# Moving the adds of complex products from VectorE into accumulating matmuls, with wider table operations and a new load order, in a state-space layer with a gated unit

## The chip, the cores and the metric

The kernel runs on one core of one Trainium2 chip. The metric is the device time of one execution in microseconds (us); medians of several executions are quoted. Engines: PE is TensorE (PEld is its weight loads), DVE is VectorE, ACT is ScalarE, POOL is GpSimd, SP issues transfers.

## The reference

A layer norm, a diagonal state-space convolution over 2048 steps for 512 channels with 128 complex states, a residual, then a second layer norm and a gated unit (ReGLU) with its residual. What matters here:

```python
logdA = dt * A                      # A, B, C complex, [512, 128]
P = exp(logdA[:, :, None] * l)      # 2048 powers
K = einsum("dn,dnl,dn->dl", C, P, dt * B).real     # the convolution's kernel
y = irfft(rfft(pad(u)) * rfft(pad(K)))[:2048] + u * Dskip
h = x + y
h2 = h + (relu(n(h) @ W_gate) * (n(h) @ W_up)) @ W_down   # n: layer norm
```

The transforms are matrix products in stages. So the work has a **front** (load and normalize x, form tables of exp, sine and cosine, form the kernel K, transform u and K, multiply the spectra) and a **back** (last stage of the inverse transform, then the gated unit).

## The kernel before

The program collects its operations, and a list scheduler inside it (below, "the planner") fixes the order of each engine's instructions from prices of its own before anything is built. So every edit of an operation can move all others.

**Powers** (called in 8 blocks). A table V of 32 complex powers is made by doubling: from m powers come the next m, by a complex factor. Each level is two products and two adds on DVE:

```python
m = 1
while m < 32:
    src, dst, tmp = V[:, :, 0:m], V[:, :, m:2 * m], self.Vt[:, :, 0:m]
    s.tt(tmp, src, bc(zi), ALU.mult, "vB")
    s.tt(dst, src, bc(zr), ALU.mult, "vA")
    s.tt(dst[:, 0], dst[:, 0], tmp[:, 1], ALU.subtract, "vC")
    s.tt(dst[:, 1], dst[:, 1], tmp[:, 0], ALU.add, "vD")
    m *= 2
```

**Kernel generator** (16 units U). The table E (magnitude times sine or cosine, four products of 1024 elements a unit on DVE) meets V in 64 small matmuls:

```python
for dl in range(8):
    for ri in range(2):
        for d in range(4):
            c = 32 * (U % 2) + 8 * d + dl
            it.append((t.v(...), V[:, ri, :, c], E[:, ri, 8 * d + dl, :], ...))
s.mms(it, "kgen")
```

**Spectral product and first inverse step** (4 groups g, each in two halves of the frequencies):

```python
s.tt(Ta, Uv, Kv[:, :, 0].unsqueeze(2).to_broadcast([128, 64, 2, 16]), ALU.mult, "pA")
s.tt(Tb, Uv, Kv[:, :, 1].unsqueeze(2).to_broadcast([128, 64, 2, 16]), ALU.mult, "pB")
s.tt(Kv[:, :, 0], Ta[:, :, 0], Tb[:, :, 1], ALU.subtract, "pC")
s.tt(Kv[:, :, 1], Ta[:, :, 1], Tb[:, :, 0], ALU.add, "pD")
# ... then, for 8 columns j and two halves of the output:
it += [(o, Sv[:, 0, j], self.G1[:, 0, sl], True, False),     # Sv is the product in Kh
       (o, Sv[:, 1, j], self.G1[:, 1, sl], False, True)]     # 128 wide
s.evac(Zv[:, 64 * ih:64 * ih + 64, :, J0:J0 + 8], ..., "e_i1")
```

**Second inverse step.** Its stationary operand (the weights that PE loads) is a slice of Z, laid out `[128, 64, 2, 128]`:

```python
it.append((t.v(...), self.Z[:, i, ri], self.H[:, i, ri], False, q == 3 and ri == 1))
```

Of the kernel before, what the change touches and what calls it, by code (L numbers as in the profile page):

```python
# [8 lines left out]
FP32 = mybir.dt.float32  # L9
# [5 lines left out]
SB_BYTES = 207 * 1024  # L15
# [52 lines left out]
class Op:  # L68
    __slots__ = ("i", "engs", "cost", "body", "deps", "reads", "writes", "tiles", "tag", "tset",
                 "prio", "users", "eng", "start", "fin", "idx", "dma", "nbytes", "vc", "ndep", "sem", "wtiles",  # L70
                 "bias")


class Sched:
# [147 lines left out]
    def cost_act(self, n):  # L222
        return 185 + n * 0.833

    def cost_dve(self, n, rate):
        return 75 + n * rate
# [37 lines left out]
    def ts(self, out, a, s1, s2, op0, op1=None, tag="ts", engs=("dve",)):  # L264
# [3 lines left out]
        c = {"dve": self.cost_dve(n, r), "pool": 300 + n * 2.2}  # L268
# [18 lines left out]
    def mms(self, items, tag="mm"):  # L287
# [3 lines left out]
        for out, l, r, st, sp in items:  # L291
            n = free_elems(r)
            m = free_elems(l)
            c += max(n, 64) * 0.42 + (40 if m == 128 else 2 + 0.42 * m) * 0.7
            ins += [l, r]
            outs.append(out)
# [37 lines left out]
    def schedule(self):  # L334
        ops = self.ops
        LAT = 130.0
        for o in ops:
            o.users = []
            o.ndep = len(o.deps)
        for o in ops:  # L340
            for j in o.deps:
                ops[j].users.append(o)
            for t in o.tiles:
                t.left += 1
        for o in reversed(ops):
# [4 lines left out]
        for o in ops:  # L350
            o.prio += o.bias
# [57 lines left out]
        while n < len(ops):  # L409
# [29 lines left out]
            if cand is None:  # L439
                for o in ready["pe"][:3]:  # L440
                    for tl in o.wtiles:
                        print(o.tag, o.i, [(d.tag, d.i, {ops[j].tag: ops[j].i for j in d.deps if ops[j].eng is None}) for d in getattr(tl, "war", [])])
# [46 lines left out]
    def emit(self):  # L489
# [44 lines left out]
        for e in ("pool", "sp", "act", "dve", "pe"):  # L534
# [12 lines left out]
            starters[e](run)  # L547
L, D, N, F = 2048, 512, 128, 1376
# [3 lines left out]
def make_consts():  # L552
# [25 lines left out]
    g1 = np.zeros((64, 2, 2, 64, 2, 2))  # L578
    for g in range(2):
        g1[:, g, 0, :, 0, g] = np.cos(ph)  # L580
        g1[:, g, 0, :, 1, g] = np.sin(ph)
        g1[:, g, 1, :, 0, g] = -np.sin(ph)
        g1[:, g, 1, :, 1, g] = np.cos(ph)
    g1 = g1.reshape(128, 512)
# [14 lines left out]
    small = np.zeros((128, 128 + 128 + 128))  # L599
    small[:, 0:128] = np.eye(128)  # L600
    small[:, 128:256] = 1.0 / 512
    small[:, 256:384] = 1.0
# [5 lines left out]
class Kernel:  # L608
    def __init__(self, nc, I, out):
        self.nc, self.I, self.out = nc, I, out  # L610
        with ExitStack() as es:  # L611
# [10 lines left out]
            s.schedule()  # L622
# [3 lines left out]
    def layout(self):  # L626
# [8 lines left out]
        rC = reg(2 * (256 + 512 + 384))  # L635
# [4 lines left out]
        rVt = reg(4096)  # L640
        rMag = reg(16384)
        rTrig = reg(12288)
        rVz = reg(12288)
        rE = reg(16384)
        rS = reg(24576)
# [3 lines left out]
        rDsk = reg(1024)  # L649
# [3 lines left out]
        c = s.mem(rC, [128, 256 + 512 + 384], BF16)  # L653
        self.cc = c
        self.F1 = c[:, 0:256]
        self.G1 = c[:, 256:768].rearrange("p (r x) -> p r x", r=2)
        self.ident = c[:, 768:896]
        self.mean_w = c[:, 896:1024]
        self.ones = c[:, 1024:1152]
# [8 lines left out]
        self.Z = s.mem(rZ, [128, 64, 2, 128], BF16)  # L668

        self.V = [s.mem(rV + 8192 * i, [128, 2, 32, 64], BF16) for i in range(2)]  # L670
        self.Vt = s.mem(rVt, [128, 2, 16, 64], BF16)
        self.mag = [s.mem(rMag + 4096 * i, [128, 2, 32, 32], BF16) for i in range(4)]
        self.trig = [s.mem(rTrig + 6144 * i, [128, 3, 32, 32], BF16) for i in range(2)]
        self.vz = s.mem(rVz, [128, 12, 512], BF16)
        self.E = [s.mem(rE + 8192 * i, [128, 2, 32, 64], BF16) for i in range(2)]
        self.Eoff = [rE + 8192 * i for i in range(2)]
        self.S = [s.mem(rS + 8192 * i, [128, 32, 2, 64], BF16) for i in range(3)]
        self.Kh = [s.mem(rS + 8192 * i, [128, 32, 4, 2, 16], BF16) for i in range(3)]
        self.Tm = [s.mem(rT + 4096 * i, [128, 64, 2, 16], BF16) for i in range(2)]
# [3 lines left out]
        self.dsk = s.mem(rDsk, [128, 512], BF16)  # L683
        self.sm = rSm
        self.rS = rS
        self.par = s.mem(rT, [128, 6, 4, 128], BF16)
        self.ldt_b = s.mem(rT + 6144, [128, 512], BF16)
# [13 lines left out]
        assert rMag + 16384 - rV >= 32768  # L701
# [13 lines left out]
    def loads(self):  # L715
# [4 lines left out]
        s.generic("pool", 300, lambda e: e.memset(self.neghalf, -0.5), [self.neghalf], [], "ms")  # L720
        for g in range(2):
# [3 lines left out]
        for i, nm in enumerate(("A_A_re", "A_A_im", "A_B_re", "A_B_im", "A_C_re", "A_C_im")):  # L725
# [4 lines left out]
            if i == 1:  # L730
                s.dma(self.cc, self.cd["f1g1"][:], 128 * 2304, "cc")
# [20 lines left out]
    def prep(self):  # L752
# [8 lines left out]
        f = [s.mem(self.rS + 2048 * i, [128, 512], FP32) for i in range(12)]  # L761
# [39 lines left out]
        s.tt(self.vz[:, 0], t0, t1, ALU.add, "prep")  # L801
        s.tt(t0, wr, ms, ALU.mult, "prep")
        s.tt(t1, wp, mc, ALU.mult, "prep")
        s.tt(self.vz[:, 1], t0, t1, ALU.subtract, "prep")
# [3 lines left out]
        for m in range(5):  # L808
# [5 lines left out]
            s.evac(self.vz[:, 2 + 2 * m], br, "zcp")  # L814
            s.evac(self.vz[:, 3 + 2 * m], bi, "zcp")
# [63 lines left out]
    def vblock(self, B):  # L879
# [3 lines left out]
        s.evac(V[:, :, 0, :], self.vz[:, 0:2, sl], "v0")  # L883
        m = 1
        lev = 0
        while m < 32:
            zr = self.vz[:, 2 + 2 * lev, sl]
            zi = self.vz[:, 3 + 2 * lev, sl]

            def bc(z):  # L890
                return z.unsqueeze(1).unsqueeze(1).to_broadcast([128, 2, m, 64])
            src, dst, tmp = V[:, :, 0:m], V[:, :, m:2 * m], self.Vt[:, :, 0:m]
            s.tt(tmp, src, bc(zi), ALU.mult, "vB")
            s.tt(dst, src, bc(zr), ALU.mult, "vA")
            s.tt(dst[:, 0], dst[:, 0], tmp[:, 1], ALU.subtract, "vC")
            s.tt(dst[:, 1], dst[:, 1], tmp[:, 0], ALU.add, "vD")
            m *= 2
            lev += 1
# [12 lines left out]
    def tables_trig(self, U):  # L911
# [7 lines left out]
        s.act(tr[:, 0], t.v(), AF.Sin, tag="sin")  # L919
        s.act(tr[:, 2], t.v(), AF.Sin, bias=self.halfpi, tag="cos")  # L920
        s.ts(tr[:, 1], tr[:, 0], -1.0, None, ALU.mult, tag="neg")

    def etab(self, U):
# [4 lines left out]
        for ri in range(2):  # L928
# [196 lines left out]
```

## Time and profile before

| | before |
|---|---|
| time, median of 3 | 385.9 us (385.58 to 386.04) |
| span of the profiled execution | 384.3 us, mean granted PE clock 0.897 |
| front (to the start of the second inverse step at 239.8 us) | DVE busy 204.0, ACT 166.0, PE 129.0 |
| back (from there to the end) | PE busy 133.8 of 144.5 |

The page's first part gives busy time, share of the span and instruction count of each engine; its second part cuts the span into 40 slices and prints the busy share in tenths; its fourth part gives the shares of the chain of waits that ended last.

```profile
PE 262.8 (68%) x2885; PEld 163.4 (43%) x2904; DVE 266.9 (69%) x482; ACT 205.1 (53%) x249; POOL 5.2 (1%) x10
...
PE   0210052648445778673878599999999999999990
...
DVE  1599999999999546999999983755532741630803
...
PEclk9999999999755588985889769999999999999996
...
DVE 46%; PE 39%; issue 4%; DMA 3%; ACT 2%; ACTq 2%; POOLq 0%; POOL 0%; DVEq 0%
```

DVE is nearly full up to the 24th slice, PE from there on. In the front PE has gaps, and from the 11th to the 24th slice its granted clock reads 0.5 to 0.8 in most slices; in the first ten, where PE is nearly idle in half of them, it reads 0.9 or more.

### The profile page before, as it was taken

The page shows a single profiled execution, that of the slowest core. Times are in us where ns is not written, and L with a number is a line of the kernel's source. Part 1 is how long each engine was busy: PE and PEld are TensorE (multiplying, and loading weights), DVE is VectorE, ACT ScalarE, POOL GpSimd, SP SyncE. Part 2 cuts the span into 40 slices and gives each one's busy share as a digit, 9 for nine tenths or more (in the row PEclk, how much of TensorE's full clock was granted, in tenths as well). Part 3 has the DMA queues.
Part 4 walks back from the last instruction along what each step waited for, and adds up shares of the span by engine and source line. Part 5 has one row for each costly group of instructions (what it writes and reads, how often), then busy time and mean ns, then how long its engine had stood idle before and what let it go on. Part 6 is the DMA issues. An engine that isn't in the chain of part 4 may idle for free.

```text
span 384.3 us, 6840 instructions
## 1 busy us (share of the span) xinstructions
PE 262.8 (68%) x2885; PEld 163.4 (43%) x2904; DVE 266.9 (69%) x482; ACT 205.1 (53%) x249; POOL 5.2 (1%) x10
## 2 busy tenths in 40 slices
PE   0210052648445778673878599999999999999990
PEld 0100030326322454531768498845445544544540
DVE  1599999999999546999999983755532741630803
ACT  0256749989866378678899458443321320511201
POOL 0110000110000000000000000000000000000000
PEclk9999999999755588985889769999999999999996
DMA  5457000014450000000024981300000010010101
GB/s 129 136 162 281 6 0 1 2 25 95 96 228 0 0 2 0 3 1 0 3 90 159 367 342 33 118 0 2 0 3 0 20 36 0 18 39 2 39 17 55
DMA packets 21246, 24.10 MB, mean 63 GB/s; under 512 B 12928, under 2 KB 18656, under 8 KB 20448
## 3 DMA queue, kind: packets, MB, share of 16 engines
q1 hardware_dynamic: 20160, 22.62, 18.0%
q10 hardware_dynamic: 1056, 1.05, 0.8%
q8 instruction: 23, 0.38, 0.4%
q14 instruction: 7, 0.06, 0.0%
HBM read 17.37 MB, written 4.19 MB: 56 GB/s over the span
## 4 chain that ended last, share of the span: by engine, by line
DVE 46%; PE 39%; issue 4%; DMA 3%; ACT 2%; ACTq 2%; POOLq 0%; POOL 0%; DVEq 0%
PE psum L301 39%; DVE arena L261 37%; DVE arena L239 4%; DMA arena<-in_A_u_dram 3%; ACTq L327 2%; ACT arena L252 1%; DVE arena L821 1%; DVE arena L281 1%; DVE arena L272 1%; DVE arena L273 1%; PE psum L316 1%; ACT arena L238 1%; POOLq L611 0%; POOL arena L828 0%; ACT L252 0%
## 5 line engine op out<-in xcount | busy, mean ns | idle before, releaser
L301 PE MATMUL psum<-arena 128*32 128x64 bf16 (+6 forms) x2797 | 255.2, 274 | 90.8 <-DVE arena L261 45.7
L301 PEld LDWEIGHTS psum<-arena 128*128 128x128 bf16 (+3 forms) x2816 | 157.9, 128 | 188.1 <-DVE arena L261 46.5
L261 DVE TENSOR_TENSOR arena<-arena 128x1024 bf16<-128x1024 bf16 (+7 forms) x283 | 156.1, 606 | 3.8 <-ACT arena L238 1.2
L252 ACT ACTIVATE arena<-psum 128x1024 bf16<-128x1024 f32 (+2 forms) x92 | 72.2, 825 | 73.9 <-PE psum L301 70.5
L238 ACT ACTIVATE arena<-psum 128x1024 bf16<-128x1024 f32 (+2 forms) x89 | 77.9, 917 | 49.3 <-PE psum L301 29.3
L261 DVE TENSOR_TENSOR arena<-psum,arena 128x512 bf16<-128x512 f32 (+2 forms) x52 | 34.9, 688 | 47.5 <-PE psum L301 47.5
L239 DVE CAST arena<-psum 128x512 bf16<-128x512 f32 (+1 forms) x29 | 27.1, 947 | 30.3 <-PE psum L301 30.3
L252 ACT ACTIVATE arena<-arena 128x512 f32<-128x512 f32 (+3 forms) x25 | 18.1, 769 | 30.3 <-DVE arena L261 16.5
L316 PE MATMUL psum<-arena 128*128 128x128 bf16 x88 | 8.2, 243 | 21.5 <-DMA arena<-in_A_A_im_dram 13.5
L252 ACT ACT_TABLE_LOAD x12 | 15.4, 1283 | 9.9 <-issue 9.7
L821 DVE BATCH_NORM_STATS2 arena<-arena 128x6 f32<-128x512 bf16 x16 | 10.7, 683 | 12.2 <-DMA arena<-in_A_u_dram 12.2
L252 ACT ACTIVATE arena<-psum,arena 128x1024 bf16<-128x1024 f32 x16 | 17.5, 1116 | 1.7 <-DVE arena L261 1.7
L316 PEld LDWEIGHTS psum<-arena 128*128 128x128 bf16 x88 | 5.8, 106 | 23.4 <-DMA arena<-in_A_A_im_dram 13.5
L261 DVE TENSOR_TENSOR arena<-arena,psum 128x2048 bf16<-128x2048 bf16 x4 | 9.2, 2288 | 4.6 <-PE psum L301 4.6
L281 DVE SCALAR_TENSOR_TENSOR arena<-psum,arena 128x512 bf16<-128x512 f32 x16 | 11.1, 743 | 0.1
L238 ACT ACTIVATE arena<-arena 128x512 bf16<-128x512 f32 (+1 forms) x15 | 7.6, 518 | 5.7 <-PE psum L301 3.4
L239 DVE COPY arena<-psum 128x512 bf16<-128x512 bf16 x10 | 3.8, 410 | 9.7 <-PE psum L316 9.7
L272 DVE TENSOR_SCALAR arena<-arena 128x1024 bf16<-128x1024 bf16 (+1 forms) x20 | 7.1, 370 | 2.1 <-ACT arena L252 2.0
L828 POOL TENSOR_TENSOR arena<-arena 128x4 f32<-128x4 f32 x4 | 4.8, 1209 | 76.0 <-DVE arena L272 76.0
L273 DVE TENSOR_SCALAR arena<-arena 128x512 bf16<-128x512 bf16 x16 | 5.5, 410 | 0.0
L281 DVE SCALAR_TENSOR_TENSOR arena<-arena 128x512 f32<-128x512 f32 (+1 forms) x9 | 4.0, 446 | 0.2 <-POOL arena L828 0.2
L823 DVE BATCH_NORM_AGGREGATE arena<-arena 128x2 f32<-128x6 f32 x16 | 2.5, 174 | 0.3
(9 smaller groups left out, 2.5 us busy)
## 6 DMA issues: line engine op xcount, KB each, us to landing
arena<-const_h SPq DMA_DIRECT2D x4, 1024.0 KB, 5.8
arena<-const_m SPq DMA_DIRECT2D x4, 768.0 KB, 11.1
arena<-arena SPq DMA_DIRECT2D x32, 64.0 KB, 2.1
xd_spill<-arena SPq DMA_DIRECT2D x1, 2048.0 KB, 8.6
arena<-xd_spill SPq DMA_DIRECT2D x1, 2048.0 KB, 16.5
out_dram<-arena SPq DMA_DIRECT2D x16, 128.0 KB
arena<-in_B_W_gate_dram SPq DMA_DIRECT2D x1, 1376.0 KB, 8.8
arena<-in_B_W_up_dram SPq DMA_DIRECT2D x1, 1376.0 KB, 11.8
```

The lines of the kernel that those rows point to most:

```text
L238: return eng.activation(ap_of(out), ap_of(src), AF.Copy)
L239: return eng.tensor_copy(ap_of(out), ap_of(src))
L252: return eng.activation(ap_of(out), ap_of(src), func, **kw)
L261: return eng.tensor_tensor(ap_of(out), ap_of(a), ap_of(b), op)
L272: return eng.tensor_scalar(ap_of(out), ap_of(a), s1, s2, op0)
L273: return eng.tensor_scalar(ap_of(out), ap_of(a), s1, s2, op0, op1)
L281: return eng.scalar_tensor_tensor(ap_of(out), ap_of(a), s, ap_of(b), op0, op1)
L301: ins_ = eng.matmul(ap_of(out), l, r, start=st, stop=sp)
L316: r = eng.transpose(ap_of(out), i_, ident)
L327: return e.dma_start(out, src)
L821: s.generic("dve", 620, lambda e, k=k: e.bn_stats(self.st[:, k, :], self.x[:, k, :]), [self.st[:, k, :]], [self.x[:, k, :]], "bns")
L828: s.generic("pool", 600, lambda e, sl=sl: e.tensor_tensor(self.rs[:, sl], self.rs[:, sl], self.neghalf.to_broadcast([128, 4]), ALU.pow), [ ...
```

## The change

Its intent: DVE bounds the front, so take work from it.

- The last doubling writes its two products into two buffers (V and a new T2) and never adds them; the kernel generator runs twice as many matmuls, which accumulate both in PSUM.
- The spectral product writes both products, of all frequencies and half the columns at a time, and never adds them; the first inverse step runs four matmuls of 256 columns for each j in place of four of 128.
- The first doubling is done once for all blocks, the other adds are one instruction a level, the tables are two products of 2048 in place of four of 1024.
- The planner gets new prices and a list of priorities; among other things it decides the order of the loads.
- Z becomes `[128, 128, 128]` with the other index innermost.
- To make room, the spectra of K (S and Kh) have two buffers in place of three, and parameters and scratch share memory with other buffers.

The core of the diff (cuts marked):

```diff
     def cost_dve(self, n, rate):
-        return 75 + n * rate
+        return 155 + n * rate
...
-            s.schedule()
+            s.schedule(PRIO)
...
-        self.Z = s.mem(rZ, [128, 64, 2, 128], BF16)
+        self.Z = s.mem(rZ, [128, 128, 128], BF16)
...   (last doubling)
+            s.tt(V[:, m:2 * m]..., V[:, 0:m]..., zr, ALU.mult, "vA")
+            s.tt(self.swap(self.T2[:, m:2 * m]), V[:, 0:m], zi, ALU.mult, "vT")
...   (tables)
-        for ri in range(2):
-            s.tt(lo, m[:, 0], tr[:, 2 if ri == 0 else 1], ALU.mult, "E")
-            s.tt(E[:, ri, :, 32:64], m[:, 1], tr[:, 2 if ri == 0 else 0], ALU.mult, "E")
+        s.tt(lo, mb(m[:, 0]), tr[:, 0::2], ALU.mult, "E")
+        s.tt(E[:, :, :, 32:64], mb(m[:, 1]), tr[:, 0:2], ALU.mult, "E")
...   (kernel generator)
-            for ri in range(2):
+            for h, W in enumerate((V, self.T2)):
+                for ri in range(2):
...   (product and first inverse step)
-                    s.tt(Kv[:, :, 0], Ta[:, :, 0], Tb[:, :, 1], ALU.subtract, "pC")
-                    s.tt(Kv[:, :, 1], Ta[:, :, 1], Tb[:, :, 0], ALU.add, "pD")
...
-                        it += [(o, Sv[:, 0, j], self.G1[:, 0, sl], True, False),
-                               (o, Sv[:, 1, j], self.G1[:, 1, sl], False, True)]
+                        it += [(o, Ta[:, :, 0, j], self.G1[:, 0], True, False),
+                               (o, Ta[:, :, 1, j], self.G1[:, 1], False, False),
+                               (o, Tb[:, :, 0, j], self.G1[:, 1], False, False),
+                               (o, Tb[:, :, 1, j], self.G1[:, 2], False, True)]
...
-                    s.evac(Zv[:, 64 * ih:64 * ih + 64, :, J0:J0 + 8], ..., "e_i1")
+                    s.evac(self.Z.rearrange("p (g j) x -> p j g x", g=2)[:, J0:J0 + 4], ..., "e_i1")
...   (second inverse step)
-                               self.Z[:, i, ri], self.H[:, i, ri], False, q == 3 and ri == 1))
+                               self.Z[:, :, 2 * i + ri], self.H[:, i, ri], False, q == 3 and ri == 1))
```

## The prediction

> **What bounds the kernel now.** I read the page's slices first. VectorE (DVE) is at nine tenths or more in almost every slice up to the 25th; from there TensorE (PE) is. So there are two kernels in one: a front (state-space convolution) and a back (inverse transform, gated unit). I then cut the span into stages with the table of busy time by window:
>
> ```profile
> core 0: us, PE busy (x) PEld busy (x) DVE busy (x) ACT busy (x) POOL busy (x), PEclk, DMA share, GB/s
> 0.00:20.00 20.00, 2.43 (x16) 1.38 (x16) 7.48 (x20) 2.24 (x5) 1.35 (x7) 1.00 0.50 131
> ...
> 122.00:154.00 32.00, 22.66 (x193) 14.14 (x196) 18.84 (x22) 18.72 (x20) 0.00 (x0) 0.69 0.00 1
> ...
> 268.00:374.00 106.00, 105.01 (x594) 51.51 (x603) 42.45 (x69) 25.46 (x39) 0.00 (x0) 1.00 0.05 16
> ...
> 0.00:234.00 234.00, 123.15 (x1942) 87.59 (x1947) 203.96 (x386) 161.21 (x187) 5.18 (x10) 0.85 0.27 87
> 0.00:248.00 248.00, 136.75 (x2160) 100.71 (x2167) 210.76 (x395) 169.57 (x196) 5.18 (x10) 0.86 0.27 88
> ```
>
> In the first 234 us DVE works 204, ScalarE (ACT) 161, PE 123. DVE idles 30 us there: 12.5 in the first 20 us, 13.2 in the stretch 122 to 154, and 4.3 elsewhere. In the back PE works 105 of 106 us. The chain of waits says the same, DVE 46% and PE 39%, and the start of the chain is a load of the input until 19.9 us:
>
> ```profile
> 7.56 12.34 DMA arena<-in_A_u_dram
> ```
>
> So DVE time taken from the front shortens the kernel as long as DVE stays its bound; nothing done for DVE in the back can. The groups by shape give the price of each DVE instruction (all-bf16 tensor_tensor on 128 partitions):
>
> ```profile
> L261 DVE TENSOR_TENSOR arena<-arena 128x1024 bf16<-128x1024 bf16 x112 | 70.6, 686 | 0.6
> L261 DVE TENSOR_TENSOR arena<-arena 128x2048 bf16<-128x2048 bf16 x40 | 47.2, 1222 | 1.7 <-ACT arena L238 1.2
> L261 DVE TENSOR_TENSOR arena<-arena 128x512 bf16<-128x512 bf16 x32 | 12.2, 422 | 0.5
> L261 DVE TENSOR_TENSOR arena<-arena 128x256 bf16<-128x256 bf16 x32 | 7.9, 287 | 0.4
> L261 DVE TENSOR_TENSOR arena<-arena 128x128 bf16<-128x128 bf16 x32 | 5.7, 220 | 0.2
> L261 DVE TENSOR_TENSOR arena<-arena 128x64 bf16<-128x64 bf16 x16 | 2.3, 187 | 0.2
> ```
>
> From 1024 to 2048 elements the price grows by 536 ns, so 0.52 ns an element and about 150 ns fixed. All these groups have almost no idle time ahead of them: DVE runs them back to back.
>
> [...] The new views (a pair taken in swapped order, broadcasts, runs of 8) keep the innermost step at one, so I expect the same prices; the table product already writes with a step of minus one at 686 ns for 1024. [...] in the back a group of four 512-wide matmuls releases a reader every 0.86 us, 216 ns each[...].
>
> **The change part by part, DVE.**
> 1. Doubling of the powers (8 blocks). Before, five levels, each two products of 128, 256, 512, 1024, 2048 elements and two adds of half as many: 2 x (220+287+422+686+1222) + 2 x (187+220+287+422+686) = 9278 ns, times 8 = 74.2 us. After, the first level is done once for all blocks, three levels have two products and one joint add of 256, 512, 1024, and the last has two products of 2048 and no add: 3 x (287+422+686) + 2 x 1222 = 6629 ns, times 8 = 53.0 us. **Minus 21.2 us.** Paid for by the joint first level, three of 1024, 2.1 us, and five negations of 512 fp32 elements, which have no row of their own; between the 410 ns of a bf16 scalar op and the 685 of an fp32 tensor_tensor, 2.8 us in all. **Plus 4.9.**
> 2. Tables: 64 products of 1024 become 32 of 2048: 43.9 to 39.1. **Minus 4.8.**
> 3. Spectral product: eight times (2 x 1222 + 2 x 686) = 30.5 becomes eight times 2 x 1222 = 19.6. **Minus 11.0.**
>
> Sum minus 32.1: DVE work in the front goes from 204 to 172 us.
>
> **The change, PE.** The adds come back as matmuls. The kernel generator gets 128 instead of 64 matmuls a unit, 1024 more; the trace shows 64 of their weight loads, one for each matmul, in 1.01 us[...]:
>
> ```profile
> 139.86 1.01 PEld L301 LDWEIGHTS psum<-arena 128*32 128x32 bf16 x64 [0.21 <-ACT arena L238]
> ```
>
> So 1024 x 16 ns = plus 16 us. The inverse step keeps 256 matmuls, but 256 wide instead of 128. Now a stretch of such (with others of that width) runs 156 in 9.56 us, 61 ns each[...]. PE work before 248 us rises from 137 to about 165. ACT stays at 161: the evacuations are as many and as wide.
>
> **The change, loads.** ACT and SP issue both kinds of load at once now, and the parameters that the tables need land behind the input; the small one for the step sizes is used only at 44.9 us. Loading the parameters first lets DVE form tables and powers' bases while the input arrives. DMA moves 131 GB/s in that stage[...], so some wait stays. I give it 4 of the 12.5 us. The list of priorities also changes the order of everything, with a better price per DVE instruction in the planner (155 ns fixed, near the 150 above). That can interleave the stretch from 122 us, where DVE and ACT only pass matmul results in turn, with table work: another 4 of 13.2 us.
>
> **Sum.** DVE work 172, plus idle time: 8.5 at the start, 9 in the stretch, and 12 elsewhere instead of 4, because ACT (161) and PE (165) now fill over four fifths of the same span and two scratch buffers have become shared with PE (below). That is 201.5, or 32.5 us less than 234. The back gains nothing (PE floor). The hand-over to it loses perhaps 1 us, and a planner with better prices may win 2 in the front. 385.9 - 32.5 + 1 - 2 = about 352 us.
>
> **Rivals.**
> - *ACT or PE becomes the bound of the front.* For it: three engines at 172, 161 and 165. If they hand work to each other as badly as in the stretch 122 to 154 (DVE 19 of 32, PE clock 0.69), the front runs at four fifths: 172 / 0.8 = 215, and the kernel takes some 367. Against it: table, power and product work has its own double buffers[...].
> - *Single buffers become the wait.* The swapped products of the last level now sit in one buffer that the matmuls read, and so do both spectral products, which only DVE read before. DVE must wait for PE before it writes them again. In the last group nothing else is left to do[...]; before, from the last product at 226 to the dense matmuls at 244 it was 18, of which some 14 after the products. So about even at the end, and up to 8 x 1.5 us if the eight blocks wait. That would make 360 or so.
> - *The late loads show.* From about 207 to 233 us the spill, the inverse matrices and the gate weights come in, 9 MB, and the inverse starts 10 us later:
>
> ```profile
> 233.82 9.56 PE L301 MATMUL psum<-arena 128*128 128x128 bf16 x156 [0.83 <-DVE arena L261]
> ```
>
> If the front's last group shortens by more than those 10 us, PE would wait for these loads, for up to 5 us.
> - *The plan is simply much better.* At 95% of DVE from 8 us on: 172 / 0.95 + 8 = 189, kernel 341.
> - [...]
>
> **Range and chances.** 352, with 338 (the better plan and a little more) to 365 (rivals one or two) for 8 in 10. For less than 2% gain 25 of the 32 us would have to be lost in new waits; I give that 4%, and slower by over 2% 1%. Faster by over 2%: 95%.
>
> **What would show each step right or wrong.** In the changed kernel: DVE busy total down by about 32 us (266.9 to 235), with tensor_tensor rows of 2048 elements still at 1222 ns[...]. PE busy up by some 28. First long DVE run before 12 us. GLU part (dense 512-wide matmuls) still about 136 us long. The waits DVE on PE in the front under 10 us; more would be rival two, and waits of PE on the late loads rival three. The prediction is wrong if the front shortens by under 20 us while DVE loses its 32: then idle time came in its place.

What is cut said things of the hardware that no trace or run of this case shows. Terms of the forecast went with it. PE's plus 28 was plus 16 for the generator, which stands, and plus 12 for the inverse step, whose price for a matmul of 256 columns was not a measured one; so 12 us of the 165 (137 + 16 + 12) stand on a cut term, and with them a part of the 12 us of idle time "elsewhere". The same price made the "about 13 us" of the last group in the second rival, against the 14 that it gives the kernel before. Its 1.5 us a block is the author's guess. The sum came to about 352 us, with these terms in it.

## More of the kernel before

The record marks every execution as fast or slow. Only fast ones are compared; one of s3_dve_less (384.28 us, the other three 378.54 to 381.39) was slow and is left out of the ratios.

## The result

The changed kernel is correct and takes **396.7 us** (median of 4, 394.89 to 398.38) against 386.0 us of the kernel before (median of 4, with one more run than in the table above, 385.58 to 386.29). All runs were fast ones. A ratio is the mean time of one kernel's fast runs over that of the other's of the same rounds, so not quite the ratio of the medians: here 1.0278, 95% interval 1.0232 to 1.0324. The change made the kernel slower by 2.8%.

Where a difference in us is given below between two experiments, it is the difference of their ratios to the kernel before, times 385.5 us, because experiments ran on several chips, each beside the kernel before. The intervals are mostly 0.3% to 0.7% on either side, so such a difference is good to 2 or 3 us.

The same parts of the page, of the changed kernel:

```profile
PE 291.7 (74%) x3928; PEld 198.5 (50%) x3928; DVE 246.1 (62%) x358; ACT 215.8 (55%) x259; POOL 6.3 (2%) x11
...
PE   0035030389857888579886867998999999999995
...
DVE  1569999999789979889952231397334424324432
...
PEclk9999999989986989688968998999999999999999
...
PE 54%; DVE 19%; ACT 15%; issue 4%; DMA 4%; ACTq 2%; POOL 1%; DVEq 0%
```

DVE lost 20.8 us and PE gained 28.9. Yet the front did not end sooner: PE's own full stretch begins no earlier (26th slice in place of the 24th), and DVE's 21st to 24th slices read 5, 2, 2, 3 where they read 9, 9, 9, 8 before: at the end of the front DVE now waits. The chain of waits went over from DVE (46% to 19%) to PE and ACT.

The table of busy time by window (start and end, length, then busy us and instructions of PE, PEld, DVE, ACT and POOL, granted clock, DMA share, GB/s) puts numbers on it. Before:

```profile
0.00:24.00 24.00, 3.04 (x20) 1.73 (x20) 11.41 (x29) 3.94 (x8) 2.36 (x8) 1.00 0.47 127
...
46.00:78.00 32.00, 15.04 (x244) 8.62 (x244) 31.34 (x75) 24.94 (x28) 1.38 (x1) 1.00 0.00 1
...
0.00:239.80 239.80, 128.95 (x2035) 93.39 (x2040) 203.96 (x386) 165.97 (x192) 5.18 (x10) 0.85 0.26 86
239.80:384.30 144.50, 133.82 (x853) 70.04 (x866) 62.97 (x96) 39.15 (x58) 0.00 (x0) 0.98 0.07 24
```

After:

```profile
0.00:24.00 24.00, 1.86 (x8) 1.01 (x8) 8.13 (x20) 1.49 (x2) 2.07 (x7) 1.00 0.53 146
...
46.00:78.00 32.00, 7.55 (x40) 5.02 (x40) 31.31 (x55) 16.79 (x25) 1.10 (x1) 1.00 0.47 132
...
200.00:222.00 22.00, 17.21 (x412) 15.31 (x401) 9.50 (x9) 10.76 (x13) 0.00 (x0) 0.82 0.78 287
...
0.00:244.85 244.85, 148.35 (x3064) 119.77 (x3065) 181.82 (x277) 161.40 (x188) 6.27 (x11) 0.91 0.28 90
244.85:394.90 150.05, 143.37 (x864) 78.68 (x864) 64.25 (x81) 54.38 (x71) 0.00 (x0) 1.00 0.05 15
```

The last two rows of each are the front and the back, parted where PE starts the second inverse step. **Front.** DVE works 181.8 us in place of 204.0, 22.1 less. But it idles 244.85 - 181.82 = 63.0 us in place of 35.8, 27.2 more, and the front is 5.1 us longer. **Back.** 150.05 us in place of 144.5, 5.5 more. Together that is the 10.6 us between the two spans. So two questions are open: why the front gave back all that DVE saved and more, and why the back, whose arithmetic hardly changed, got longer.

The chain of waits at the change from front to back of the changed kernel (start, duration, what):

```profile
195.91 2.73 issue
198.63 11.27 PE psum L306 x363
209.90 3.54 issue
213.44 6.46 PE psum L306 x97
219.91 2.37 DVE arena L261 x2
...
222.34 7.42 PE psum L306 x128
229.78 2.37 DVE arena L261 x2
...
232.20 3.73 PE psum L306 x32
235.95 2.37 DVE arena L261 x2
...
238.37 5.38 PE psum L306 x32
243.77 1.03 ACT arena L238
...
244.85 8.39 PE psum L306 x76
253.27 6.12 DVE arena L261
```

Two products on DVE (2.37 us), then matmuls that read them, then again two products: from 219.9 us on the two engines take turns: the product's two buffers are single, and DVE's wait ends each time with matmuls. DVE's list of waits in the stretch from 170 to 245 us has one large line (engine and line, what it waited for: us in total, times, longest):

```profile
DVE arena L261 <- PE psum L306: 23.9, 4, 10.2
```

Four waits, 23.9 us: the first product instruction of a half (10.2, 7.5 and 3.8 us in the last three). Added up over the front by operation, that instruction's waits come to 1.4 us in the kernel before and to 24.8 here.

The chain has one more thing, "issue": time in which PE waits for nothing that the profile shows. PE's list of waits has one line of it, and the page's list of DMA queues has one of the kind `instruction`:

```profile
PE psum L306 <- issue: 10.5, 6, 3.5
...
q8 instruction: 31, 0.51, 0.5%
```

The 31 packets of that queue, 16 KB each, are the 0.51 MB. All six waits end 1.3 to 1.5 us after one of these packets landed (the last two, 2.73 and 3.54 us long, end at 198.63 and 213.44 us; the packets landed at 197.11 and 212.09). Over all runs 66 of the 76 such waits over 0.3 us end 1.2 to 1.6 us after one; by chance it would be some 4% of them (an estimate: 31 packets times 0.4 us in some 310 us). That PE waits there for its next instructions is the author's reading; no run was made to test it. The kernel before, with 2885 matmuls in its profile in place of 3928, has 23 such packets and 1.9 us of this wait.

In the back, two groups changed that the diff did not touch. Before, then after (line, engine, operation, tile, shapes, count, then busy us, mean ns, idle time before them):

```profile
L261 DVE TENSOR_TENSOR arena<-arena,psum 128x2048 bf16<-128x2048 bf16 x4 | 9.2, 2288 | 4.6 <-PE psum L301 4.6
...
L252 ACT ACTIVATE arena<-arena 128x2048 bf16<-128x2048 bf16 x4 | 7.6, 1910 | 15.1 <-PE psum L301 12.2 <-DVE arena L261 3.0
```

```profile
L261 DVE TENSOR_TENSOR arena<-arena,psum 128x2048 bf16<-128x2048 bf16 x4 | 15.7, 3933 | 15.2 <-PE psum L306 15.2
...
L252 ACT ACTIVATE arena<-arena 128x2048 bf16<-128x2048 bf16 x4 | 10.0, 2532 | 1.3 <-DVE arena L261 1.3
...
L261 DVE TENSOR_TENSOR arena<-arena 128x2048 bf16<-128x2048 bf16 x72 | 85.2, 1220 | 33.6 <-PE psum L306 30.7 <-ACT arena L238 2.1 <-ACT arena L252 0.2
```

The mean subtraction (first line) takes 1.7 times as long, and the square (second) 1.3 times, at the same shapes. The third line answers a question that the new views raise: the products of 2048 elements still take 1220 ns (1222 before), so these views did not slow them.

### The profile page after: what moved, and what is told of

Read it like the earlier page. It is cut to its first block, busy times and chain, and to the rows that moved or that the text cites. A ratio compares the mean times of both kernels' runs of the same rounds, so it can differ in the third digit from the quotient of the medians.

```text
span 394.9 us, 8819 instructions
## 1 busy us (share of the span) xinstructions
PE 291.7 (74%) x3928; PEld 198.5 (50%) x3928; DVE 246.1 (62%) x358; ACT 215.8 (55%) x259; POOL 6.3 (2%) x11
## 4 chain that ended last, share of the span: by engine, by line
PE 54%; DVE 19%; ACT 15%; issue 4%; DMA 4%; ACTq 2%; POOL 1%; DVEq 0%
PE psum L306 54%; DVE arena L261 13%; ACT arena L252 9%; ACT arena L238 4%; DMA arena<-in_A_u_dram 4%; ACT L252 2%; ACTq L332 2%; DVE arena L239 2%; DVE arena L875 1%; DVE arena L281 1%; DVE arena L273 1%; POOL arena L882 1%; DVE arena L272 1%; PE psum L321 0%; DVE arena L877 0%
## 5 line engine op out<-in xcount | busy, mean ns | idle before, releaser
L306 PE MATMUL psum<-arena 128*32 128x64 bf16 (+5 forms) x3840 | 284.3, 263 | 79.6 <-DVE arena L877 21.4
L306 PEld LDWEIGHTS psum<-arena 128*32 128x32 bf16 (+2 forms) x3840 | 192.7, 139 | 169.8 <-issue 35.1
L261 DVE TENSOR_TENSOR arena<-arena 128x2048 bf16<-128x2048 bf16 (+6 forms) x166 | 130.4, 823 | 36.1 <-PE psum L306 30.7
L252 ACT ACTIVATE arena<-psum 128x1024 bf16<-128x1024 f32 (+2 forms) x92 | 73.3, 824 | 81.0 <-PE psum L306 79.2
L238 ACT ACTIVATE arena<-psum 128x1024 bf16<-128x1024 f32 (+2 forms) x105 | 92.6, 951 | 44.4 <-PE psum L306 43.2
L252 ACT ACTIVATE arena<-arena 128x512 f32<-128x512 f32 (+3 forms) x25 | 20.8, 879 | 17.1 <-DVE arena L261 15.3
L261 DVE TENSOR_TENSOR arena<-arena,psum 128x2048 bf16<-128x2048 bf16 x4 | 15.7, 3933 | 15.2 <-PE psum L306 15.2
L239 DVE CAST arena<-psum 128x1024 bf16<-128x1024 f32 (+1 forms) x18 | 20.3, 1149 | 1.7 <-PE psum L306 1.7
L875 DVE BATCH_NORM_STATS2 arena<-arena 128x6 f32<-128x512 bf16 x16 | 10.8, 686 | 15.8 <-DMA arena<-in_A_u_dram 15.6
L252 ACT ACT_TABLE_LOAD x10 | 12.8, 1283 | 10.9 <-issue 10.7
L321 PEld LDWEIGHTS psum<-arena 128*128 128x128 bf16 x88 | 5.9, 108 | 21.4 <-DMA arena<-in_A_C_im_dram 14.7
L272 DVE TENSOR_SCALAR arena<-arena 128x1024 bf16<-128x1024 bf16 (+2 forms) x25 | 9.3, 380 | 1.0 <-ACT arena L252 0.7
L238 ACT ACTIVATE arena<-arena 128x256 bf16<-128x256 bf16 (+1 forms) x11 | 5.6, 515 | 0.0
L239 DVE CAST arena<-arena 128x512 bf16<-128x512 f32 x5 | 2.0, 421 | 0.0
## 6 DMA issues: line engine op xcount, KB each, us to landing
arena<-in_B_W_gate_dram SPq DMA_DIRECT2D x1, 1376.0 KB, 10.1
```

Of the source, the lines that this page charges most:

```text
L238: return eng.activation(ap_of(out), ap_of(src), AF.Copy)
L239: return eng.tensor_copy(ap_of(out), ap_of(src))
L252: return eng.activation(ap_of(out), ap_of(src), func, **kw)
L261: return eng.tensor_tensor(ap_of(out), ap_of(a), ap_of(b), op)
L272: return eng.tensor_scalar(ap_of(out), ap_of(a), s1, s2, op0)
L306: ins_ = eng.matmul(ap_of(out), l, r, start=st, stop=sp)
```

## The experiments

The theory at the start: (1) the back is longer because Z's new layout makes the weights of the second inverse step 256 bytes apart; (2) the front did not shorten because DVE and PE hand work to each other, so DVE's time was not at full worth and PE's not free. The rivals: the planner's new order alone did it; the later loads did it.

### The layout of Z: e1_z_rows

The changed kernel, with Z stored so that the weights lie side by side again; the evacuation now writes with the large step.

```diff
-  s.evac(self.Z.rearrange("p (g j) x -> p j g x", g=2)[:, J0:J0 + 4], ...)
+  s.evac(self.Z.rearrange("p x (g j) -> p x g j", g=2)[:, :, :, J0:J0 + 4], ...)
-  self.Z[:, :, 2 * i + ri]
+  self.Z[:, 2 * i + ri]
```

> The changed kernel with one layout put back: the 128 weights of a column of Z lie side by side in memory again, where the change laid them 256 bytes apart. Theory (weights at a wide step load slowly[...]): the 192 matmuls of the inverse go from 107 ns back to about 61 each, the mean subtraction beside them from up to 6.1 us back to 2.3, and the kernel loses 9 to 12 us, to 385 to 388. Rival (the inverse is slow because the new order leaves it nothing to overlap with, and the layout is free): the inverse stays at 107 ns a matmul and the time stays at 395 to 398.

Measured: 386.4 us, ratio 1.0022 (0.9962 to 1.0083), so 9.9 us less than the changed kernel. The timeline of PE at the start of the second inverse step, in the changed kernel and then here (start, duration, engine, line, operation, count):

```profile
244.85 15.36 PE L306 MATMUL psum<-arena 128*128 128x128 bf16 x140 [1.12 <-ACT arena L238]
```

```profile
243.85 9.06 PE L306 MATMUL psum<-arena 128*128 128x128 bf16 x148 [1.16 <-issue]
...
L261 DVE TENSOR_TENSOR arena<-arena,psum 128x2048 bf16<-128x2048 bf16 x4 | 9.1, 2286 | 12.3 <-PE psum L306 12.1
```

15.36 / 140 is 110 ns for a matmul with its weight load, 9.06 / 148 is 61 ns, each with some 512 columns wide among them (216 ns from start to start). Without those, the 192 matmuls of the changed kernel's second inverse step start 102 ns apart in the mean, and that is a mean of two kinds: of every twelve four have weights of another tensor, side by side in both kernels, and follow each other at 56 ns; the eight with weights from Z take 125 ns in the mean. 128 of these at 69 ns more are 8.8 us. And with the weights side by side the mean subtraction beside them is back at 2286 ns, the square at 1919. Why DVE and ACT took longer beside the wide step (3933 and 2532 ns), the runs do not show; POOL has nothing to do in the back (0.00 us). The back of this run is 139.8 us long, 10.3 less than in the changed kernel, and 4.7 less than in the kernel before: PE is busy there for 134.2 us (before 133.8) and idles for 5.6 in place of 10.7. The new order runs the second inverse step in one go where the old one mixed it with the gated unit, which is the likely reason. The front (243.9 us) is as long as in the changed kernel.

The planner made another order here too (DVE's and ACT's instructions differ from about 183 us on), so the 9.9 us are not the layout's alone. The durations are: e2 and e4 below, again two layouts in an order of their own, have the first mean subtraction at 4.96 and 2.29 us and the first square at 5.79 and 1.90. What the layout is worth in the time of the kernel depends on the order, as e4 shows.

### The planner: e2_no_prio, e3_before_planner, e4_z_rows_no_prio, f4_old_planner

e2 is the changed kernel without the list of priorities (`s.schedule()` in place of `s.schedule(PRIO)`); e3 is the kernel before with the new prices and the list; e4 is e1 without the list; f4 is e1 with the old prices and without the list.

> The changed kernel with the list of priorities emptied (the planner's new prices stay). If the new order is what keeps DVE's saved 25 us from showing (x tiles late at the start, gated unit held back until the inverse is over), it gets faster by 5 us or more, below 392. If the order is as good as it can be and PE and ACT are simply the new bound, it gets slower or stays within 3 us of 396.7.

> The kernel before with the new planner only: its prices and its list of priorities, no change of the arithmetic or the buffers. If the order and the loads are worth something by themselves it is below 384; if they cost, above 388. It tells the part of the planner from that of the arithmetic.

> Both: weights side by side and no priorities. If the two effects are separate, its time is that of the changed kernel plus the two differences of the single edits, to within 3 us. If the gated unit's overlap with the inverse is what the order changes, the layout is worth less here than alone (under 6 us)[...].

> Base 386.4. The planner of the kernel before (its prices, no list of priorities) on the new arithmetic. The planner on the arithmetic of before cost 9.5 us. If it costs the same here, this run is at 377, and DVE's saving shows in part. If the list was made for the new arithmetic and serves it, this run is at 395 or above, like the one with new prices and no list (400.6).

| run | us | ratio to before |
|---|---|---|
| e2_no_prio | 394.0 | 1.0229 (1.0184 to 1.0274) |
| e3_before_planner | 394.4 | 1.0248 (1.0204 to 1.0291) |
| e4_z_rows_no_prio | 400.6 | 1.0407 (1.0369 to 1.0444) |
| f4_old_planner | 395.5 | 1.0242 (1.0195 to 1.0289) |

The list does little for the changed kernel (2 us, intervals that overlap), costs the arithmetic of before 9.6 us, and gains 14.8 us for e1 (e4 has the same prices and no list). So the order alone is worth some 10 to 15 us either way, and its effect is not a sum of parts: by the sum of the parts e4 should have come to some 384 us, and without the list the kernel with the weights side by side is 6.9 us slower (e4 against e2), although its instructions are no longer slow. The planner's own estimate, printed when the kernels are built, does not tell it: it puts e3 at 415 us, before at 407, the changed kernel at 380 and e1 at 385. Any experiment that lets the planner reorder mixes its edit with such a shift.

### Undoing the moves, reordered: f1_undo_a, f2_undo_b, g1_old_product

f1 is e1 with the last doubling's add back on DVE; f2 is e1 with the product's adds back; g1 also goes back to the product by halves of the frequencies.

> Base: the changed kernel with Z's rows put back (386.4). The adds of the last doubling go back to DVE: 512 matmuls... counted out: 1024 matmuls of 16 ns leave PE (17 us), eight adds of 2048 elements (1180 ns apart) come to DVE (9.4 us). Theory (PE and its hand-overs bound the front, DVE's time there is worth nothing any more): the same as the base within 3 us, or up to 8 faster. Rival (DVE still bounds the front): 5 to 9 us slower.

> Base 386.4. The adds of the spectral product go back to DVE (16 of 1024 elements, 630 ns apart, 10 us) and 128 of the 256 matmuls of 256 columns leave PE[...]; the product buffers are again read by DVE alone, so that DVE need not wait for PE. Theory (PE bounds, and the last group is a chain of product, matmuls, product, matmuls): 2 to 8 us faster. Rival (DVE bounds): 5 to 10 slower.

> Same base, right result. The spectral product goes back to halves of its rows with the adds on DVE (so a half needs half of the group's second-step matmuls, and only DVE uses the scratch buffers); the inverse step stays 256 wide with 128 matmuls. In the base the first product of a part waits 14.0 us in all, 24.8 in the changed kernel, 1.4 in the kernel before. If that wait is what eats the saving of the product's adds, this is 4 to 8 us faster than the base, at 378 to 382, and beats both kernels. If the wait only sits in a chain that is as long either way, within 3 us of 385.

Measured: f1 392.2 us (1.0176, 1.0159 to 1.0194), f2 385.0 us (0.9970, 0.9936 to 1.0004), g1 388.9 us (1.0102, 1.0035 to 1.0169). In all three the planner made another order. Against e1 they are 5.9 us slower, 2.0 us faster (within the intervals) and 3.1 us slower. They settle nothing by themselves, as the pinned runs below show.

### The order of the loads: f3_params_first

e1 with the remaining parameters' loads raised in the list, ahead of most of x.

```diff
-    'cc': 122000, ... 'ldtb': -86000, ... 'par2': -238000, 'par3': -388000, 'par4': -628000, 'par5': -172000,
+    'cc': 525000, ... 'ldtb': 503000, ... 'par2': 515000, 'par3': 512000, 'par4': 509000, 'par5': 506000,
```

> Base 386.4. Only the order of the loads: all six parameters, the step sizes and the constants before the input tiles (the change put just the first two there and held four back to 22 to 56 us; the powers' base was ready at 78 us, before at 43). Theory (PE starts late because the powers come late, and from then on three engines have equal work left): PE's work in the first 78 us rises from 17 us, and the kernel is 5 to 15 us faster. Rival (the start is hidden behind the bound of the later stages): within 3 us.

Measured: 390.1 us, ratio 1.0131 (1.0098 to 1.0164), 4.2 us slower than e1, which neither forecast had. DVE does idle less in the first 78 us, 16.1 in place of 19.0 us, so that part did what it should; the rest of the order moved with it. The worth of the loads by themselves stays open.

### What a microsecond of each engine is worth: s1_act_less, s2_pe_less, s3_dve_less

These keep e1's order exactly and shorten single instructions. Their outputs are wrong, which doesn't matter for the times. s1 runs the sine and cosine activations on a quarter of the columns, s2 leaves out the 1024 added matmuls of the kernel generator, s3 runs the table products on half the rows. Each operation keeps its place, its price for the planner and its waits; s1 and s3 (and h1 below) also fill buffers on POOL, 5 to 7 us. (The values left out in s2 are small; it is still not the function.)

```diff
-        s.mms(it, "kgen")
+        half = [x for n in range(8) for x in it[16 * n:16 * n + 8]]     # V's products alone
+        s.mms(it, "kgen", real=half)                                    # s2
...
-        s.tt(lo, mb(m[:, 0]), tr[:, 0::2], ALU.mult, "E")
+        s.tt(lo, mb(m[:, 0]), tr[:, 0::2], ALU.mult, "E", real=(... 16 of 32 rows ...))   # s3
```

> Wrong result on purpose. Base: changed kernel with Z's rows back (386.4), every engine's order the same. Only the 32 sine and cosine activations work on a quarter of their columns: 20.5 us less for ACT in the front, nothing else changed. If ACT bounds the front's middle (rival one of the prediction), 10 to 18 us faster. If the front's length is its chain of hand-overs, under 5 us.

> Wrong result on purpose. Same base, same order. The 1024 added generator matmuls (those of the swapped products) are left out: 16.4 us less for PE. If PE bounds the front: 10 to 16 us faster. If ACT does: under 4. If each generator stands in the chain of hand-overs but not back to back, between, some 0.5 us a unit, 4 to 8.

> Wrong result on purpose. Same base, same order. The 32 table products work on half of their rows: 17 us less for DVE. The prediction took DVE's time in the front at full worth: 12 to 17 us faster. If DVE's saving has been worth little since the change: under 5.

| run | us | ratio to before | engine's busy time against e1 | time against e1 | worth |
|---|---|---|---|---|---|
| s1_act_less | 378.2 | 0.9823 (0.9782 to 0.9863) | ACT 204.8 to 185.5 | -7.7 | 0.40 |
| s2_pe_less | 373.4 | 0.9704 (0.9637 to 0.9770) | PE 285.4 to 269.1 | -12.3 | 0.75 |
| s3_dve_less | 381.2 | 0.9880 (0.9820 to 0.9940) | DVE 242.3 to 226.0 | -5.5 | 0.34 |

The worth is us of time for each us of the engine, good to perhaps 0.2. s2 is where PE as the bound was expected; s1 and s3 lie between their two forecasts. In e1 a microsecond of PE is worth about twice one of DVE: the change moved work from the engine that had come to matter less to the one that matters more. A part of PE's worth may be its "issue" waits, which fall from 6.3 us in e1 to 1.2 in s2. Counted with them, s2 relieves PE of 21.4 us, at 0.57 each.

### Undoing the moves at a fixed order: p1_undo_a_pinned, p2_undo_b_pinned, p3_undo_ab_pinned

e1's order of every engine and its PSUM banks are written out as a table and replayed; an added DVE instruction goes right behind its products. p1 puts the last doubling's add back, p2 the product's, p3 both. All three are correct.

```diff
-            s.schedule(PRIO)
+            s.replay(ORDER)
...   (p1, p3)
+            s.tt(vf, vf, self.T2[:, m:2 * m].rearrange("p a r d -> p (a r d)"), ALU.add, "vF")
-            for h, W in enumerate((V, self.T2)):
+            for h, W in enumerate((V,)):
...   (p2, p3)
+                s.tt(Kv[:, :, 0, js], Ta[:, :, 0], Tb[:, :, 1], ALU.subtract, "pC")
+                s.tt(Kv[:, :, 1, js], Ta[:, :, 1], Tb[:, :, 0], ALU.add, "pD")
-                it += [ ... four matmuls on Ta and Tb ... ]
+                it += [ ... two matmuls on Kv ... ]
```

> e1 with the last doubling's adds back on the vector engine (half of the doubling's matmuls gone), everything else in e1's order on every engine. If the worths found at fixed order add up (tensor engine 0.8, vector engine 0.3 us per us): about -8 us of matmuls x 0.8 = -6 (up to -13 if as s2) and +9 us of adds x 0.3 = +3, so 374 to 384 us. If the moves themselves were right and only the order was at fault: 387 to 396 us.

> e1 with the product's adds back on the vector engine (half of the first inverse step's matmuls), e1's order. Worths of 0.8 and 0.3: about -8 x 0.8 + 10 x 0.3 = -3, so 378 to 386 us. Move right: 388 us or more.

> e1 with both groups of adds back on the vector engine, e1's order. Worths of 0.8 and 0.3: 368 to 382 us, below both e1 and the kernel before. If vector time becomes the bound once 20 us are put back: 388 to 400 us.

| run | us | ratio to before | against e1 | PE busy against e1 | DVE busy against e1 |
|---|---|---|---|---|---|
| p1_undo_a_pinned | 381.5 | 0.9910 (0.9874 to 0.9945) | -4.3 | -10.7 | +9.1 |
| p2_undo_b_pinned | 380.3 | 0.9878 (0.9846 to 0.9909) | -5.6 | -10.8 | +9.8 |
| p3_undo_ab_pinned | 380.9 | 0.9877 (0.9830 to 0.9923) | -5.6 | -18.4 | +19.0 |

Undoing either move gains, and undoing both gains no more than undoing one. The trade itself is about one to one: between p3 and e1, 19.0 us of DVE for 18.4 us of PE. So, by these runs, it can gain only while PE has time to spare. s2 and p1 leave out the same 1024 matmuls, and p1 has 9.7 us more of DVE (251.3 against 241.6) and is 7.9 us slower (0.9910 less 0.9704): with PE relieved, DVE's time is worth about 0.8 again, good to 0.3. The worth of an engine's time changes with each move.

p1 and f1 have the same arithmetic, and 0.9910 against 1.0176 is 10.3 us from the planner's order alone. That is why f1 seemed to clear the moves.

The waits of DVE fall with the moves undone. The group of 2048-element products in e1, then in p3:

```profile
L261 DVE TENSOR_TENSOR arena<-arena 128x2048 bf16<-128x2048 bf16 x72 | 85.4, 1221 | 21.9 <-PE psum L306 14.3 <-ACT arena L238 6.7 <-ACT arena L252 0.2
```

```profile
L261 DVE TENSOR_TENSOR arena<-arena 128x2048 bf16<-128x2048 bf16 x80 | 95.0, 1222 | 7.6 <-ACT arena L238 6.5
```

In e1 these products wait 14.3 us for PE; in p3 that wait is not in the list any more, and DVE idles 241.89 - 204.24 = 37.7 us in the front, about what it did before (35.8).

### DVE and PE time in the kernel before: h1_before_dve_less, n2_before_pe_more, n1_before_traded

Results are wrong. h1 keeps the order of the kernel before and runs its table products on half the rows. n2 only adds matmuls: every one of the kernel generator twice, three in place of two at the first inverse step. n1 is n2 with the 32 adds of 1024 elements that the change moves shrunk to 64 elements: the change's trade, without its single buffers.

n2 and n1 were meant to keep that order too, and do not. The loop that they add at the first inverse step (not in the cut below) uses the name `st`, which counts the loop around it. So half of Z's columns are never written, the planner sees other dependences and makes another plan: of the evacuations of 1024 elements DVE has 10 in place of 14 and ACT 70 in place of 66. (Built with another name there, which was not run, n2 gets the plan of before in every position.) Between themselves n2 and n1 have one order.

```diff
   (n1, n2)
+        more = []
+        for o, l, r, st, sp in it:
+            more += [(o, l, r, st, False), (o, l, r, False, sp)]
-        s.mms(it, "kgen")
+        s.mms(it, "kgen", real=more)
   (n1)
-                    s.tt(Kv[:, :, 0], Ta[:, :, 0], Tb[:, :, 1], ALU.subtract, "pC")
+                    s.tt(Kv[:, :, 0], Ta[:, :, 0], Tb[:, :, 1], ALU.subtract, "pC",
+                         real=(Kv[:, q, 0], Ta[:, q, 0], Tb[:, q, 1]))      # q: 4 of 64
```

> The kernel before with its table products done on half the rows (wrong result on purpose), vector engine about -17 us, order the same. The prediction's theory (vector engine is the bound of the front at full worth): 368 to 371 us. Rival (dependencies shared by three engines, worth about 0.3 to 0.5): 377 to 381 us.

> The kernel before at its own order with only matmuls added: every matmul of the last table product twice (1024 more), three in place of two at the first inverse step (128 more), about 24 us of tensor time; wrong result on purpose. If tensor time is hidden beside the vector engine there, as the prediction assumed: 385 to 389 us. If the engines share one chain of dependencies: 393 us (0.35 per us) or more, up to 404 us at a worth of 0.8.

> As n2_before_pe_more, and the 32 adds of 1024 elements that the change moves shrunk to 64 elements each (about 16 us of vector time less), order unchanged, wrong result on purpose: the change's trade at the order of the kernel before. Prediction's theory (vector time worth 0.85, tensor time free): 371 to 375 us. Rival, the trade gains nothing anywhere because the tensor engine sits in the same chain: 382 us or more.

| run | us | ratio to before | DVE busy | PE busy | time against before |
|---|---|---|---|---|---|
| h1_before_dve_less | 370.2 | 0.9613 (0.9582 to 0.9643) | 266.9 to 250.0 | 262.8 to 261.0 | -14.9 |
| n2_before_pe_more | 386.3 | 1.0019 (0.9977 to 1.0061) | 266.9 to 262.6 | 262.8 to 273.1 | +0.7 |
| n1_before_traded | 380.1 | 0.9870 (0.9838 to 0.9903) | 266.9 to 246.8 | 262.8 to 274.1 | -5.0 |

h1: in the kernel before, DVE time is worth 14.9 / 16.9 = 0.88, nearly full, as the prediction had it. n2: 0.7 us for 10.3 us of PE looks as if PE's time were free there, as the prediction had it; but DVE has 4.3 us less to do, which at 0.88 would be worth 3.8 us. So PE may have cost up to 4.5 us, and free is not shown. n1 against n2, in one order: with the matmuls in place, the adds taken away are worth only 0.0149 x 385.5 = 5.7 us for 262.6 - 246.8 = 15.8 us of DVE, or 0.36 (good to 0.15). n1's time, too, lies between its two forecasts.

The timelines show where the rest stays. The first mean subtraction on DVE, in before, h1, n2 and n1:

```profile
244.57 2.29 DVE L261 TENSOR_TENSOR arena<-arena,psum 128x2048 bf16<-128x2048 bf16 x1 [0.46 <-PE psum L301]
```

```profile
228.71 2.29 DVE L262 TENSOR_TENSOR arena<-arena,psum 128x2048 bf16<-128x2048 bf16 x1 [0.46 <-PE psum L302]
```

```profile
246.21 2.29 DVE L261 TENSOR_TENSOR arena<-arena,psum 128x2048 bf16<-128x2048 bf16 x1 [0.46 <-PE psum L301]
```

```profile
239.25 2.29 DVE L262 TENSOR_TENSOR arena<-arena,psum 128x2048 bf16<-128x2048 bf16 x1 [0.46 <-PE psum L302]
```

h1 reaches it 15.9 us earlier than before, n1 7.0 earlier than n2. And the last product instructions of n2, then of n1, run here:

```profile
224.14 7.42 DVE L261 TENSOR_TENSOR arena<-arena 128x2048 bf16<-128x2048 bf16 x8 [0.75 <-ACT arena L238]
```

```profile
217.16 5.42 DVE L262 TENSOR_TENSOR arena<-arena 128x2048 bf16<-128x2048 bf16 x8 [1.02 <-ACT arena L238]
```

DVE is done at 222.6 in place of 231.6 us, 9.0 earlier; from there to the mean subtraction it takes 16.7 in place of 14.7 us (in the kernel before 10.8). So of the 15.8 us taken from DVE, 6.8 go to waits before its last product, and 2.0 to PE's work behind it, which nothing hides.

## Why the prediction was wrong

**The account.** From the kernel before to the changed one in three steps, each with a run at its end:

| step | run | time against the run above |
|---|---|---|
| everything but the moved adds and the layout of Z (wider operations, prices, list, loads), at e1's order | p3_undo_ab_pinned | -4.7 |
| both moves of adds, order kept | e1_z_rows | +5.6 |
| Z at 256-byte steps | the changed kernel | +9.9 |

The sum is +10.8 us, the measured +10.7. It is one path; with other orders the steps differ (n1, in its own order, has the moves at -5.0; from e4 to e2 the wide step of Z is worth -6.9). The third step contains a new order as well, the first the two buffers for the spectra in place of three.

**The step that failed** is the sentence "So DVE time taken from the front shortens the kernel as long as DVE stays its bound", together with the idle time in the sum. The first half was true of the kernel before (h1: 0.88), but DVE did not stay the bound. The sum had DVE work of 172 and 29.5 us idle; measured were 181.8 and 63.0. The prediction named the sign of its own failure in its last sentence: idle time came in DVE's place. What took over is its first rival, and PE (worth 0.75, or 0.57 with its "issue" waits) more than ACT (0.40) and DVE (0.34, all in e1), with a part of its second, the single buffers, in the waits of the first product (24.8 us). How much the single buffers cost apart from PE's plain load was not tried on its own: a second T2 takes 8 KB and second product buffers another 8, and nothing that size is free in this layout. Nor were PE's "issue" waits (10.5 us in the changed kernel, none over 0.3 us in p3), which the prediction does not have.

In its second rival one reading is off: before, 10.0 us lie between the end of DVE's last product instruction (233.8) and the dense matmuls (243.7), not 14; and the last group's 13 us were 15.1 (229.8 to 244.9): the two times 32 matmuls took 3.73 and 5.38 us in the chain above.

**The size of DVE's saving.** Predicted 32.1 us; measured 24.6 (266.9 to 242.3 in e1, which has no slowed operations). The mis-sized term is the price of one instruction. The mean durations (1222, 686, 187 ns for 2048, 1024, 64 elements) overlap when instructions run back to back; busy time over count in the rows that the prediction shows is 47.2 / 40 = 1180, 70.6 / 112 = 630 and 2.3 / 16 = 144 ns. With these spacings the doubling saves 18.1 us in place of 21.2, the tables 2.6 in place of 4.8 and the product 10.1 in place of 11.0; less about 5 for the preparation, that is near 26.

**PE, plus 28.** The total is right by luck, 28.9, for its parts are not: 6.3 of it came with the wide step of Z (e1 has 285.4), and the moved adds make 18.4 in place of 28 (e1 against p3), 12 of which stood on the cut price. The generator's 1024 are priced right (18.1 to 33.5 us, plus 15.4). That PE's time is hidden in the kernel before is not shown (n2); that it is not free once DVE is relieved, s2 shows (0.75). One part of the small rise may be the clock: matmuls of three shapes that the moves do not touch take 6.9 us less in e1 than in p3, whose order is the same, and the granted clock of the front is 0.90 in e1 and 0.81 in p3 (0.85 before, 0.91 in the changed kernel). What sets the clock, the runs do not show: in the first 46 us of the kernel before it reads 1.00, with PE busy for 3.65 us.

**"The back gains nothing (PE floor)."** It lost 5.5 us: e1's back is 4.7 us shorter than before, likely by the new order, and the weights' step, with the order that came with it, added 10.3. No step of the prediction looked at the layout of Z, one line of the diff. The dense matmuls of the gated unit kept their length; the second inverse step and what ran beside it did not.

**The loads: minus 4 at the start.** The sign was wrong. In the first 24 us DVE works 8.1 us in place of 11.4, and the generator's first matmuls start at 101 in place of 68 us, because four of the six parameters are now loaded behind most of x (in the window from 46 to 78 us loads still move 132 GB/s, before 1). With the parameters first (f3) the matmuls start at 78 us again. The change's words were taken for what the planner would do with them. What this costs the kernel is open (f3).

**The planner: minus 2, and 4 in the stretch from 122 us.** There was no basis for either. On the arithmetic of before, the new prices and the list cost 9.6 us (e3).

**Right as told:** 1220 ns for the new views; no wait of PE on late loads at the second inverse step; the gated unit's length.

**The best version** found is p2_undo_b_pinned: the last doubling's adds as matmuls, the product's adds on DVE, Z with its rows together, e1's order. 380.3 us, 1.2% less than the kernel before (0.9846 to 0.9909) and 3.9% less than the changed one; p1 and p3 are within a microsecond or so of it.

## What to carry to other kernels

Before moving work off the bounding engine, ask what the receiving engine's time will be worth after the move, not before it: measure it by shortening single instructions at a fixed order (a wrong result is fine for that), and expect a trade of one to one to stop paying as soon as the two are level (here both moves together cost 5.6 us at e1's order). PE's busy share is no sign of a gain: it rose from 68% to 74%, and that of its weight loads from 43% to 50%, while the kernel became 2.8% slower. Look at the "issue" waits of many small matmuls too: PE's rose from 1.9 to 10.5 us with the change. When a planner sits in the kernel, pin its order for every comparison and check in the trace that it stayed, or its shifts (10.3 us between p1 and f1) will be read as the effect of the edit. Check the innermost step of every operand that a change lays out anew, above all of matmul weights (125 ns a matmul in place of 56 with Z at 256-byte steps), also in stages whose arithmetic it leaves alone.
